# Handing a hand-synchronised section to GpSimd without its drain, and turning the two waits of the last stores

## The chip, the cores and the metric

The kernel runs on one core of one Trainium2 chip. The metric is the time of one execution in microseconds (us) as the device measures it. It was measured in several rounds, each beside the kernel before on the same chip. The time of a run is about 1.75 us more than the span of its trace (575.02 against 573.27 in the profiled run of the kernel before). In the records shown here, us and ns count from the start of the span.

## The reference

With a 1x1 depthwise kernel, the program is a scale per channel followed by a matrix product over 147,456 pixels of 384 channels:

```python
# x: (1, 384, 384, 384) bf16, dw: (1, 1, 384), pw: (384, 384)
out = x * dw[0, 0][None, None, None, :]
return jnp.einsum('bhwc,cd->bhwd', out, pw)
```

## The kernel before

The scale is folded into the weights at the start (the "head"): a 0/1 selection matrix times `dw`, then matmuls with `pw` (line 243), then six evictions into `w_r` (line 299; an eviction copies matmul results out of `ps`, where TensorE leaves them). After that TensorE runs 288 supertiles of 48 matmuls each in one loop (line 193). VectorE transposes x ahead of it, ScalarE evicts the results behind it, and SyncE issues nearly all loads and stores. Everything stands in one section in which the author sets every semaphore by hand:

```python
    with tc.tile_critical():                      # line 104: entry and exit of the section
        ...
        def store(t, k):
            ...
            if first + 1 == NS:                   # the last supertile: two half stores
                je = first
                part = slice(2 * D * k, 2 * D * k + 2 * D)
                nc.sync.wait_ge(s_a[je % 2], je // 2 + 2 + k)   # ScalarE's quarter
                nc.sync.wait_ge(s_d, k + 1)                     # VectorE's quarter, line 143
                nc.sync.dma_start(dst[:, part], src[:, part]).then_inc(s_o[g % NR], 16)
                return
```

The head keeps TensorE busy with matmuls on zeros, and repeats some folding matmuls. Both are there only to raise TensorE's clock in time:

```python
        nc.tensor.wait_ge(s_zero, 1)
        idle_work(3)                              # 12 matmuls on zeros
        ...                                       # three tiny matmuls that spread dw
        idle_work(3)
        nc.tensor.wait_ge(s_pw, 16)
        times = {(1, 1): 3, (2, 0): 2}            # repeats of the folding pairs (k, r)
        for k in range(3):
            nc.tensor.wait_ge(s_sw, k + 1)
            for r in range(2):
                if k == 2:
                    nc.tensor.wait_ge(*w_done[r])
                for v in [0, 1] * times.get((k, r), 1):
                    mm = nc.tensor.matmul(...)    # line 243
                mm.then_inc(s_w)                  # releases one eviction into w_r
```

The last supertile's eviction is shared by two engines:

```python
            if jj + 1 == NS:
                nc.vector.wait_ge(s_o[g % NR], ...)     # an older store of this buffer
                nc.vector.wait_ge(s_pe, 2 * jj + 2)     # the matmuls
                nc.scalar.wait_ge(s_pe, 2 * jj + 2)
                for q in (0, 2):
                    nc.scalar.copy(Ov[:, q, j, :], PS[s][:, q, :D]).then_inc(s_a[s])
                    nc.vector.tensor_copy(Ov[:, q + 1, j, :], PS[s][:, q + 1, :D]).then_inc(s_d)
```

## Time and profile before

| what | before |
|---|---|
| time, median of the first 3 runs | 575.13 us (575.04 to 575.19) |
| head: start to the loop's first matmul | 6.98 us |
| loop: first to last matmul's start | 561.46 us |
| tail: last matmul's start to the end of the span | 4.84 us |
| last store's landing to the start of GpSimd's exit barrier | 0.707 us |

Read it as three pieces one after the other. The loop is TensorE at work without a gap, so a change that doesn't touch it can only win in the head or in the tail. The profile lines for this stand in the prediction. The finer steps come from the trace's records of single sequencer instructions; each gives a start in ns.

### The profile page before, as it was taken

The numbers are of one execution on the slowest core, as the hardware profiler recorded it, in microseconds if no ns is written. First come the engines' busy times: TensorE is split into PE (matmuls) and PEld (weight loads), VectorE is DVE, ScalarE is ACT, GpSimd is POOL, SyncE is SP. The second block draws the span as 40 slices with busy tenths as digits, with TensorE's granted clock in tenths as the row PEclk, the third lists the DMA queues.
The fourth block names the chain that finished last, engine by engine and source line by source line (L and its number), as shares of the span: only waits on it lengthen the run. The fifth ranks groups of instructions, "written<-read, shape, count | busy, mean of one in ns | idle before, by whom it ended". The sixth has DMA issues, their size and how long they took to land.

```text
span 573.3 us, 29723 instructions
## 1 busy us (share of the span) xinstructions
PE 566.7 (99%) x13869; PEld 411.9 (72%) x13869; DVE 507.4 (89%) x584; ACT 419.0 (73%) x297; POOL 0.9 (0%) x8
## 2 busy tenths in 40 slices
PE   8999999999999999999999999999999999999996
PEld 5777777777777777777777777777777777777774
DVE  7898898898889889889888988988988898898895
ACT  6777777777777777777777777777777777777775
POOL 0000000000000000000000000000000000000000
PEclk9999999999999999999999999999999999999999
DMA  9999999999999999999999999999999999999676
GB/s 363 418 340 438 415 425 432 446 412 425 428 413 412 406 389 427 402 379 405 431 389 397 412 416 386 406 409 416 406 391 422 405 394 396 424 398 368 263 288 238
DMA packets 26453, 226.88 MB, mean 396 GB/s; under 512 B 1226, under 2 KB 6987, under 8 KB 22603
## 3 DMA queue, kind: packets, MB, share of 16 engines
q1 hardware_dynamic: 25264, 225.61, 97.1%
q10 hardware_dynamic: 1178, 1.18, 0.6%
q14 instruction: 10, 0.07, 0.0%
q8 instruction: 1, 0.02, 0.0%
HBM read 113.54 MB, written 113.25 MB: 396 GB/s over the span
## 4 chain that ended last, share of the span: by engine, by line
PE 97%; DMA 1%; ACT 1%; DVE 0%; issue 0%; SPq 0%
PE ps L193 97%; DMA pw_n<-in_pw_dram 1%; DMA out_dram<-O 0%; ACT w_r L299 0%; ACT O L336 0%; DVE O L334 0%; PE ps L243 0%; SPq L369 0%; SPq L104 0%
## 5 line engine op out<-in xcount | busy, mean ns | idle before, releaser
L193 PE MATMUL ps<-w_r,T 32*128 32x384 bf16 x13824 | 561.8, 321 | 0.5 <-ACT w_r L299 0.5
L286 DVE STREAM_TRANSPOSE T<-X 128x384 uint32<-128x384 uint32 x572 | 500.7, 877 | 55.4 <-DMA X<-in_x_dram 0.3
L336 ACT CAST O<-ps 128x1536 bf16<-128x1536 f32 x287 | 413.0, 1439 | 147.1 <-PE ps L193 147.1
L193 PEld LDWEIGHTS ps<-w_r,T 32*128 32x128 bf16 x13824 | 410.0, 93 | 152.3 <-issue 0.9
L299 ACT CAST w_r<-ps 128x768 bf16<-128x768 f32 x5 | 3.6, 819 | 1.1 <-PE ps L243 1.1
L210 PE MATMUL ps<-zero 32*128 32x384 bf16 x24 | 2.6, 494 | 1.4 <-POOL zero L259 1.4
L286 DVE STREAM_TRANSPOSE T<-Xl 128x384 uint32<-128x384 uint32 x4 | 3.5, 877 | 0.4
L334 DVE CAST O<-ps 128x384 bf16<-128x384 f32 x2 | 1.0, 553 | 3.1 <-DMA out_dram<-O 3.1
L271 ACT ACT_TABLE_LOAD x1 | 1.3, 1283 | 1.9 <-issue 1.9
L210 PEld LDWEIGHTS ps<-zero 32*128 32x128 bf16 x24 | 0.7, 99 | 2.6 <-issue 2.6
L243 PE MATMUL ps<-pw_n,sel_w 64*128 64x384 bf16 x18 | 2.3, 422 | 0.1
L243 PEld LDWEIGHTS ps<-pw_n,sel_w 64*128 64x128 bf16 x18 | 1.0, 121 | 1.4 <-issue 0.7
L304 DVE TENSOR_REDUCE sel<-eye 128x64 f32<-128x128 bf16 x1 | 0.3, 290 | 1.8 <-POOL eye L261 1.8
L299 DVE CAST w_r<-ps 128x768 bf16<-128x768 f32 x1 | 1.0, 958 | 1.0 <-PE ps L243 1.0
L333 ACT CAST O<-ps 128x384 bf16<-128x384 f32 x2 | 0.9, 482 | 0.5 <-PE ps L193 0.5
L314 DVE TENSOR_SCALAR sel_w<-sel,dw_f 128x256 bf16<-128x256 f32 x3 | 0.9, 347 | 0.0
L311 DVE COPY dw_f<-ps 128x3 f32<-128x3 f32 x1 | 0.2, 161 | 0.7 <-PE ps L225 0.7
L225 PEld LDWEIGHTS ps<-ones,dw_row 1*128 1x128 bf16 x3 | 0.2, 98 | 0.2 <-issue 0.2
L261 POOL TENSOR_SCALAR_AFFINE_SELECT eye<-ones 128x128 bf16<-128x128 bf16 x1 | 0.3, 294 | 0.1
L271 ACT COPY warm<-warm 128x1 f32<-128x1 f32 x2 | 0.3, 189 | 0.0
L259 POOL MEMSET zero<- 128x192 uint32 x1 | 0.3, 258 | 0.0
L225 PE MATMUL ps<-ones,dw_row 1*128 1x1 bf16 x3 | 0.2, 160 | 0.0
(6 smaller groups left out, 0.7 us busy)
## 6 DMA issues: line engine op xcount, KB each, us to landing
X<-in_x_dram SPq DMA_DIRECT2D x26, 3840.0 KB, 21.5
out_dram<-O SPq DMA_DIRECT2D x26, 3840.0 KB, 27.4
X<-in_x_dram SPq DMA_DIRECT2D x3, 1536.0 KB, 17.5
out_dram<-O SPq DMA_DIRECT2D x4, 768.0 KB, 9.3
out_dram<-O SPq DMA_DIRECT2D x2, 1536.0 KB, 14.6
X<-in_x_dram SPq DMA_DIRECT2D x3, 768.0 KB, 7.3
X<-in_x_dram SPq DMA_DIRECT2D x1, 2304.0 KB, 19.2
out_dram<-O SPq DMA_DIRECT2D x1, 2304.0 KB, 10.9
```

The lines of the kernel that those rows point to most:

```text
L193: mm = nc.tensor.matmul(PS[s][:, q, :D], lhsT=Ts[s][32 * q : 32 * q + 32, b, par::2], rhs=w_r[32 * q : 32 * q + 32, b, par, :], start=(b, ...
L210: nc.tensor.matmul(PS[0][:, i, :D], lhsT=zero[32 * i : 32 * i + 32, 0:P], rhs=zero[32 * i : 32 * i + 32, :], start=True, stop=True, tile_p ...
L225: mm = nc.tensor.matmul(PS[1][:, 0, D + k : D + k + 1], lhsT=dw_row[:, P * k : P * k + P], rhs=ones[0:1, 0:1], start=True, stop=True,)
L243: mm = nc.tensor.matmul(PS[(k + 1) % 2][:, 2 * r + v, :D], lhsT=sel_w[64 * v : 64 * v + 64, k, r, :, :].rearrange("p q w -> p (q w)"), rhs ...
L259: nc.gpsimd.memset(zero[:].bitcast(U32), 0).then_inc(s_zero)
L271: c = nc.scalar.copy(warm[:, s + 1 : s + 2], warm[:, 0:1])
L286: ins = nc.vector.transpose(out=Tw[:, 3 * h : 3 * h + 3], in_=Xw[:, :, j, 96 * h : 96 * h + 96].rearrange("p k (b w) -> p b k w", w=32),)
L299: o = nc.vector.tensor_copy(out, in_) if e == 0 else nc.scalar.copy(out, in_)
L314: nc.vector.tensor_scalar_mul(sel_w[:, k], sel[:].unsqueeze(2).to_broadcast([P, 2, 4, 32]), dw_f[:, k : k + 1]).then_inc(s_sw)
L333: nc.scalar.copy(Ov[:, q, j, :], PS[s][:, q, :D]).then_inc(s_a[s])
L334: nc.vector.tensor_copy(Ov[:, q + 1, j, :], PS[s][:, q + 1, :D]).then_inc(s_d)
L336: a = nc.scalar.copy(Ov[:, :, j, :], PS[s][:, :, :D])
```

## The change

The intent is to take synchronisation off the end of the program. GpSimd, idle after 2 us, becomes the section's synchronising engine, the one that announces the section's end and collects the answers. Its drain at the section's end is left out; a drain is the instruction with which an engine answers such an announcement. Of the two waits ahead of each last half store, the one for VectorE (which finishes last) is to be the one that the store itself carries.

```diff
-    with tc.tile_critical():
+    with tc.tile_critical(sync_engine=mybir.EngineType.Pool, no_gpsimd_drain=True):
...
                 part = slice(2 * D * k, 2 * D * k + 2 * D)
+                nc.sync.wait_ge(s_d, k + 1)
                 nc.sync.wait_ge(s_a[je % 2], je // 2 + 2 + k)
-                nc.sync.wait_ge(s_d, k + 1)
                 nc.sync.dma_start(dst[:, part], src[:, part]).then_inc(s_o[g % NR], 16)
```

The built program puts the wait written first at the store and the other one in an instruction ahead of it.

## The prediction

> **What bounds the kernel now.** I read the page first, then the chain of waits in order of time, then the records of the first 7 us and the last 5 us one instruction at a time, because the change touches only instructions at the two ends of the program.
>
> The page says which engine sets the length:
>
> ```profile
> span 573.3 us, 29723 instructions
> PE 566.7 (99%) x13869; PEld 411.9 (72%) x13869; DVE 507.4 (89%) x584; ACT 419.0 (73%) x297; POOL 0.9 (0%) x8
> PEclk9999999999999999999999999999999999999999
> PE 97%; DMA 1%; ACT 1%; DVE 0%; issue 0%; SPq 0%
> ```
>
> TensorE is busy for 99% of the span at the full granted clock, and 97% of the chain that ended last is TensorE. GpSimd does 0.9 us of work, all of it in setup. The chain in order of time then splits the span into three parts:
>
> ```profile
> 0.79 0.01 SPq L104
> ...
> 0.86 0.03 SPq L369
> ...
> 1.02 3.02 DMA pw_n<-in_pw_dram
> ...
> 4.09 0.52 PE ps L243 x2
> ...
> 4.63 2.21 ACT w_r L299 x3
> ...
> 6.98 557.90 PE ps L193 x13728
> ...
> 568.88 1.01 DVE O L334 x2
> ```
>
> Columns: start, length, what. There is a head of 6.98 us (a marker on SyncE's sequencer, then a branch that waits for it, then the load of the weights, their folding, two evictions); 557.90 us of the matmul loop in one piece, to which the chain view adds the last supertile (TensorE's last matmul ends near 568.76); and a tail of about 4.5 us. No line of the loop is touched by the diff. So the question is only how the head and the tail move, each at most a few tenths of a microsecond.
>
> The tail, from the timeline (start, length, engine, what):
>
> ```profile
> 568.80 0.86 ACT L333 CAST O<-ps 128x384 bf16<-128x384 f32 x2 [0.51 <-PE ps L193]
> 568.87 1.02 DVE L334 CAST O<-ps 128x384 bf16<-128x384 f32 x2 [3.09 <-DMA out_dram<-O]
> 569.52 0.82 SPq L144 DMA_DIRECT2D out_dram<-O  x2
> ```
>
> ScalarE and VectorE evict two quarters each, and SyncE stores them in two halves. VectorE ends later. ("DMA out_dram<-O" as the releaser of VectorE is the view's choice among two waits; that buffer's older store had landed long before, the matmuls released it.) The section's boundary is line 104:
>
> ```profile
> L104 SPq EVENT_SEMAPHORE  x3: 17/27/28, 572.2 to 572.4; - x3
> L104 SPq NOP  x2: 13/16/18, 0.8 to 572.5; - x2
> L104 POOLq DRAIN  x1: 41/41/41, 572.2 to 572.2; - x1
> L104 SPq DRAIN  x1: 7/7/7, 572.3 to 572.3; - x1
> ```
>
> Numbers are ns (least, median, most), then first and last start. The reader should see that GpSimd's drain takes 41 ns and starts together with those of the other engines.
>
> The records of single instructions, in ns resolution, give the steps I use below. SyncE's tail: wait for VectorE's first quarter 569.460, store 569.518 (344 ns); wait for the second 569.924, store 569.978; its last byte lands 571.948; the wait for it ends 571.971; branch 572.013; then the boundary: signal 572.178, drain 572.271, two waits 572.350 and 572.420, NOP 572.486, end drain 572.559, second end drain 572.622, which lets GpSimd's exit barrier go at 572.655. From its start there 0.62 us of barrier and semaphore clearing follow.
>
> **What the Trainium skill says.** "Perfetto Trace Analysis", Sequencer-only Instruction (DRAIN, etc): a record covers execution alone; the wait and the propagation of a semaphore lie outside. The trace agrees: the signal at 572.178 lasts 17 ns, and ScalarE's drain that waits for it starts at 572.217, 22 ns after. So I count starts to starts, not busy times. The same page, Identifying Dependency Chains, says that an instruction that waits on several engines may get EventSemaphore instructions ahead of it: here, the second wait of each last store is such a record on SyncE, line 143. "VectorE: DVE Perf Modes", The DRAIN you can't avoid, calls the drains of pre- and postamble constant at about 12 ns; here 7 to 17 ns on four engines and 41 ns on GpSimd, so GpSimd's is dearer but small. "DMA: Bandwidth & Descriptors", Anatomy of one DMA, gives a fixed cost near 2.0 us per DMA (fitted on GpSimd's path); the last store takes 1.97 us here, and the change leaves it alone: only its start can move.
>
> **The change part by part.** The instruction order shows no difference on TensorE, VectorE and ScalarE apart from which semaphore releases their boundary; only GpSimd and SyncE change.
>
> 1. *The two last stores.* In the kernel before, the built program has VectorE's wait in the separate instruction and ScalarE's at the store, the reverse of the source order; the changed source turns this round. VectorE is the late one: its first quarter ends 568.874 + 0.558 = 569.432, ScalarE's at 569.284. Now the store starts 569.518 - 569.432 = 86 ns after VectorE, of which 58 ns are from the separate wait to the store. With VectorE's wait at the store itself the wait for ScalarE is served early. A store that waits at itself shows what is left: the one at line 147 starts at 568.319, some 20 ns after its eviction. So 569.455, about 60 ns earlier. The second half: VectorE ends 569.897, and SyncE, 62 ns (gap 569.862 to 569.924) after the first store, is free at 569.80 + 0.06 for ScalarE's wait and at 569.92 for the store, just as VectorE's signal arrives. So about 569.92 instead of 569.978. Gain 0.055 us, straight on the path: landing and all after it follow.
>
> 2. *The exit.* Before, SyncE announces the end of the section, every engine drains and answers, SyncE collects. In the changed program GpSimd announces, right after its setup at about 2 us; the others answer as soon as each ends its own work (TensorE near 568.8, the evictors near 569.9). When SyncE comes out of its branch at 572.178 its drain finds the announcement already there. It saves the announcement: 572.271 - 572.178 = 93 ns. Then SyncE executes two waits (added by the compiler) and the end drain; before, two waits, a NOP and the end drain. It saves the NOP: 66 to 73 ns. New sum on SyncE: drain 572.178, then 79 + 70 + 66 + 63 ns by the same gaps, second end drain at 572.456 instead of 572.622: 0.165 us. GpSimd's part runs beside it: its wait sees SyncE's drain at about 572.21, its NOP about 66 ns later, the signal back at 572.32, before SyncE's end drain at 572.393 asks for it. That is a margin of 70 ns. The GpSimd drain itself gives nothing: it ended 572.261, and SyncE asked for it at 572.486.
>
> 3. *The entry.* Before, GpSimd's release of the start barrier (0.680) goes to SyncE (0.721), whose NOP (0.786) releases all branches; SyncE's own branch follows at 0.862 and its first load at 1.020. In the change GpSimd runs the NOP itself at about 0.680 + 0.07 = 0.75, the signal is out near 0.79, and SyncE, with one instruction less, reaches its branch at 0.786. So its branch starts 0.07 us sooner. That load (the weights) heads the chain: landed 4.04, first folding matmul 4.09. TensorE had been waiting since 3.87, so it can follow by 0.07; ScalarE's three evictions follow one another from there; the first transpose ends 6.684, 150 ns before the last eviction that the loop waits for (6.833), so it doesn't take over. ScalarE's load of x moves by only 0.03. Gain 0.07 us if the load's landing does not wander.
>
> Sum: 0.055 + 0.165 + 0.07 = 0.29 us of 575.13, 0.05%.
>
> **The rivals.** (a) A new wait replaces the old: GpSimd answers slower than SyncE, or SyncE's two added waits come on top. For it: five of the sequencer steps now lie on GpSimd, whose waits (572.655 to 572.733, 79 ns) are a little longer than SyncE's. Against it: 70 ns of margin. If it eats the exit gain, 575.0; if the added waits cost their whole 0.14 us with nothing saved, 575.15. (b) The entry gain vanishes, since the loop's start hangs on a DMA landing whose 16 parts are spread over 3.669 to 4.040, and on the clock's rise in the head (first full-speed record at 5.57): 574.9. (c) The drain of GpSimd hides more than its record shows: as its name in the change suggests, someone expected a gain. Nothing in the trace supports it (one 41 ns record, off the path); it would bring 574.7. (d) A big effect in the loop, through another phase of loads against stores: TensorE has 0.5 us of recorded idle time before the loop's matmuls in all, so there is nothing to win, and the loads run ahead by three buffers, so I see nothing to lose.
>
> **Range and chances.** 575.13 - 0.29 = 574.84. The three runs of before spread over 0.15 us, as large as any one of my terms; the low end takes all gains plus that spread, the high end takes no gain at all: 574.55 to 575.15. A 2% step is 11.5 us, more than head and tail together could give short of removing both, so "within 2%" is all but certain; I leave 0.015 for a state or a mechanism that I don't see.
>
> **What would show it.** Right: the loop's first matmul near 6.91 instead of 6.98; the first of the two last stores within 30 ns of the end of VectorE's first quarter, with the wait of line 143 served before that; from the last landing to GpSimd's exit barrier 0.54 us instead of 0.71; the drain of line 104 gone from GpSimd, and TensorE's drain of that line near 568.9. Wrong: a SyncE end drain that starts late after its waits (GpSimd's answer binds), a weights load that starts earlier but lands no sooner, a second store that starts no earlier although the first did, or any difference in the length of the matmul loop larger than these 0.29 us.

## The result, and the profile after

| | before | changed |
|---|---|---|
| median of 6 runs | 575.12 us | 575.02 us |
| lowest to highest | 575.04 to 575.70 | 574.78 to 576.34 |
| ratio | | 1.0001 (0.9988 to 1.0014) |

Ratios here are the mean time of one kernel's fast runs over that of the other's of the same rounds, so not quite the ratio of the medians. Within 2% it is the same, as forecast. Of the forecast 0.29 us, the medians show 0.10 and the means nothing, and two of the six runs (575.43, 576.34) lie above the forecast range, which ended at 575.15. The 0.10 is no sign of the gain: six runs with this scatter can give such a difference by chance.

The page of the changed kernel looks the same at the top:

```profile
span 573.2 us, 29725 instructions
PE 566.9 (99%) x13869; PEld 415.0 (72%) x13869; DVE 508.0 (89%) x584; ACT 419.0 (73%) x297; POOL 0.9 (0%) x8
```

The chain of waits in order of time (start, length, what) is another one in the head:

```profile
0.76 0.01 POOLq L104
...
1.14 0.20 POOL zero L259
...
1.45 1.36 PE ps L210 x12
...
2.88 1.17 PE ps L210 x12
4.05 2.05 PE ps L243 x12
6.09 0.02 issue
6.12 0.81 ACT w_r L299
6.92 0.14 issue
7.06 557.91 PE ps L193 x13728
```

Before, the chain ran over the weights' load (3.02 us), two folding matmuls (0.52) and three evictions of ScalarE in a row (2.21). Now the view takes it over TensorE's own warm-up matmuls and twelve folding matmuls (2.05), and only one eviction is on it. Its part before the folding is a matter of the view: the folding again started 47 ns after the weights' landing, as before. The part after it is real. The loop starts at 7.06 instead of 6.98 although the load came sooner: it was issued at 0.954 instead of 1.020 and landed at 3.956 instead of 4.040, and the first folding matmul started at 4.003 instead of 4.087. Somewhere between folding and loop 0.17 us were lost (3.058 us instead of 2.890).

In the tail the steps came out as worked out. The timeline (start, length, engine, what):

```profile
568.89 0.86 ACT L333 CAST O<-ps 128x384 bf16<-128x384 f32 x2 [0.51 <-PE ps L193]
568.96 1.02 DVE L334 CAST O<-ps 128x384 bf16<-128x384 f32 x2 [3.09 <-DMA out_dram<-O]
569.54 0.84 SPq L144 DMA_DIRECT2D out_dram<-O  x2
```

Everything is 0.085 us later than before (568.89 for 568.80), but the store only 0.027 (569.545 for 569.518). The instructions of line 104 (engine, kind and count, then least/median/most ns, then first and last start):

```profile
L104 POOLq NOP  x3: 13/13/13, 0.8 to 572.3; - x3
...
L104 PEldq DRAIN  x1: 1072/1072/1072, 567.8 to 567.8; - x1
L104 ACTq DRAIN  x1: 892/892/892, 568.9 to 568.9; - x1
L104 DVEq DRAIN  x1: 1009/1009/1009, 569.0 to 569.0; - x1
L104 SPq DRAIN  x1: 7/7/7, 572.2 to 572.2; - x1
```

GpSimd's drain is gone. The drains of the other engines now start while they are still at their last work: those of TensorE, ScalarE and VectorE take some 0.9 to 1.1 us, where before all stood at 572.2 and took 8 to 17 ns. The time of a drain is not a cost in itself; it lies beside the stores. By single records:

| step | before | forecast | changed |
|---|---|---|---|
| VectorE's first quarter ends, to the first half store | 86 ns | 20 to 30 | 28 |
| VectorE's second quarter ends, to the second half store | 81 ns | about 25 | 28 |
| last landing to GpSimd's exit barrier | 707 ns | about 540 | 535 |
| last matmul's start to the end of the span | 4.837 us | 4.62 | 4.632 |

So the tail won 0.205 us of the 0.22 that were forecast. The head gave 0.084 back instead of winning 0.07, which leaves 573.27 - 573.15 = 0.12 us in the two spans.

### The profile page after: what moved, and what is told of

Read it like the earlier page. It is cut to its first block, busy times and chain, and to the rows that moved or that the text cites. A ratio compares the mean times of both kernels' runs of the same rounds, so it can differ in the third digit from the quotient of the medians.

```text
span 573.2 us, 29725 instructions
## 1 busy us (share of the span) xinstructions
PE 566.9 (99%) x13869; PEld 415.0 (72%) x13869; DVE 508.0 (89%) x584; ACT 419.0 (73%) x297; POOL 0.9 (0%) x8
## 4 chain that ended last, share of the span: by engine, by line
PE 98%; DMA 0%; ACT 0%; issue 0%; DVE 0%; DVEq 0%; POOL 0%; POOLq 0%
PE ps L193 97%; PE ps L210 0%; DMA out_dram<-O 0%; PE ps L243 0%; ACT O L336 0%; ACT w_r L299 0%; DVE O L334 0%; DVEq L104 0%; POOL zero L259 0%; POOL warm L258 0%; PE ps L225 0%; POOLq L369 0%; POOLq L358 0%; POOLq L104 0%
```

## The experiments

**The theories.** A: the head's length hangs on when TensorE's full clock is granted (the trace records from when to when it was; I call the start of that record the clock's rise). The record of the granted clock begins at 5.57 us in the profile of before and at 5.92 in that of the change; both last 566.612 us, which is 166 times 3.4133 us; in the other profiles here it lasts 563.199, 570.026 or 573.439 us, so whole steps of 3.413. The Trainium skill, "TensorE: Matmul & The Clock Gate", Part 1: The HAM clock gate (the "warmup" mystery), says that the clock is released after a busy window of 3413 ns, and that the window is free-running: it doesn't reset when a kernel starts. The granted stretches agree. If so, the rise is a matter of chance in each run, and its scatter covers a gain of 0.2 to 0.3 us. B: the scatter comes from transfers or from the loop. C: GpSimd gives back elsewhere what it wins. D: what is won is the drain.

### The stretched head: e1 and e2

To take the chance out, the head was made some 4.7 us longer, so that the clock is up before the folding begins. VectorE's first reduction runs 16 times, each waiting for the one before; TensorE's second warm-up loop has 16 passes.

```diff
-        nc.vector.tensor_reduce(out=sel[:], ...).then_inc(s_dwf)
+        for n in range(16):
+            ins = nc.vector.tensor_reduce(out=sel[:], ...)
+            if n > 0:
+                ins._wait_ge(s_pad, n)
+            ins.then_inc(s_pad if n < 15 else s_dwf)
...
         mm.then_inc(s_df)
-        idle_work(3)
+        idle_work(16)
```

e1 is the kernel before with this edit:

> The kernel before with the head stretched by some 4 us: 16 small VectorE reductions in a row instead of one hold the folding back, and TensorE's second warm-up loop has 16 passes instead of 3, so that the full clock is granted before the folding matmuls begin. Theory A (the head's length depends on when the full clock is granted: 5.57 us in the profile of before, 5.92 in that of the change, and in other runs later; that scatter covers a gain of 0.2 to 0.3 us): the slow outliers go, all runs lie within 0.3 us of each other, at 578 to 581 us, and the loop's matmuls again take 561.46 us first start to last start. Theory B (the scatter comes from transfers or from the loop): the scatter stays at 0.6 us and more.

e2 is the changed kernel with it:

> The same stretched head in the changed kernel. Theory A: within 0.3 us of each other, and below the stretched kernel before by 0.22 us (the exit's 0.165 and the stores' 0.055; the entry's 0.07 is hidden behind VectorE here, whose start is the same in both). Theory B: the two can't be told apart, or differ by less than 0.1 us. Rival C (GpSimd as the synchronising engine gives back elsewhere what it wins): the changed one is no faster, 0 +- 0.05.

Measured: e1 579.70 us, five runs from 579.69 to 579.70. e2 579.51, four runs from 579.50 to 579.51 and one at 579.73. In the same rounds the unstretched kernel before scattered from 574.90 to 575.58. The clock rose at 7.77 and 6.76 us, one us apart, and it made no difference: from the first folding matmul to the loop 2.724 and 2.723 us, the loop 561.460 and 561.461. In the chain of e2, again three evictions stand in one row ahead of the loop:

```profile
8.62 0.34 PE ps L211 x4
8.96 0.01 issue
8.98 0.35 PE ps L244 x2
9.33 0.02 issue
9.35 2.21 ACT w_r L300 x3
11.57 0.14 issue
11.70 557.90 PE ps L194 x13728
```

Of theory B the loop falls, with its transfers: there nothing scatters. The loads of the head are not tested by this, since the stretch hides them as it hides the clock's rise: the weights landed at 3.995 and 3.924 us, the folding began at 8.944 and 8.979. So A fits, but these two runs alone don't part it from late loads; e10 and the table after e16 do. C falls: the change wins 0.19 us. Its parts by trace are 0.226 us in the tail (VectorE's last end to the exit barrier 2.775 and 2.549 us) less 0.034 in the head, because the loop starts at 11.702 instead of 11.668. The stretched head hangs on TensorE's warm-up loop of 16 passes: its last four matmuls (8.62, line 211) stand right ahead of the folding, while VectorE had the first selection matrix ready at 7.457, so the 16 reductions didn't bind. That loop begins 0.029 later (1.456 for 1.427), because GpSimd now runs the section's NOP before it clears the zeros. The announcement in the middle of GpSimd's setup adds nothing (the instruction after it starts 0.031 later, the one before it 0.030). The start I had put down as "same" (0.22 expected). The run at 579.73, like e5's at 579.77 below, left no trace and stays unexplained.

### The parts without the stretched head: e3 and e4

```diff
 # e3: the kernel before with the new section line alone
-    with tc.tile_critical():
+    with tc.tile_critical(sync_engine=mybir.EngineType.Pool, no_gpsimd_drain=True):
 # e4: the changed kernel with the old section line
```

> Only the section's synchronising engine and drain are changed, the order of the last waits is as before. By step: from the last landing to the exit barrier's first GpSimd wait 0.535 us (as in the change; 0.707 before); the last stores start 86 and 81 ns after VectorE's quarters (as before). Theory A: the time depends on the clock's rise in each run; the fastest run 0.24 us under the fastest of before (574.80), the median anywhere within 0.4 us of before. Rival C: the fastest run not under 575.0.

> Only the order of the last waits is changed, the section is as before. By step: the last stores start 28 ns after VectorE's quarters instead of 86 and 81; landing to exit barrier 0.707 us as before. Theory A: fastest run 0.05 us under the fastest of before (574.99), medians again not to be told apart. Rival C makes no difference here: the same.

Measured: e3 575.14 us (574.72 to 575.28), ratio 0.9997; e4 575.08 (574.88 to 576.10), ratio 1.0003. By time nothing is to be seen, as theory A has it; the fastest runs lay 0.08 and 0.11 under what was expected of them, and e3's, at 574.72, under the 575.0 of rival C. By step all came as expected: e3 0.535 us from landing to barrier and stores 87 and 82 ns after VectorE; e4 0.706 us and 28 and 27 ns.

### The parts with the stretched head: e5 to e8

Each with the stretched head: the section line alone (e5), the order of the waits alone (e6), the kernel before without GpSimd's drain (e7), the changed kernel with GpSimd's drain (e8).

```diff
 # e7, on the stretched kernel before
-    with tc.tile_critical():
+    with tc.tile_critical(no_gpsimd_drain=True):
 # e8, on the stretched changed kernel
-    with tc.tile_critical(sync_engine=mybir.EngineType.Pool, no_gpsimd_drain=True):
+    with tc.tile_critical(sync_engine=mybir.EngineType.Pool):
```

> Stretched head (before 579.70 us, changed 579.51), with only the section's engine and drain changed. Theory A, by the traces of those two: the exit gives 0.17, the section's start on GpSimd costs VectorE's first reduction 0.034 (its input comes from GpSimd, which now has one more instruction ahead of it): 579.70 - 0.17 + 0.034 = 579.56, within 0.03. Rival C (the exit gains nothing by itself, the stores' order does it): 579.70 or more.

> Stretched head, with only the order of the last waits changed. Theory A: the last store starts 28 ns after VectorE instead of 82, so 579.70 - 0.055 = 579.645, within 0.03. Rival (SyncE's own time between two stores binds, so the second store doesn't start earlier): 579.70. The sum of this and the section's run must give the whole change's 0.19 if the parts are independent.

> Stretched head; SyncE stays the synchronising engine, only GpSimd's drain is left out (a NOP takes its place). Theory A: the drain of 41 ns ended 0.2 us before SyncE asked for it: 579.70, within 0.02. Rival D (the drain is what the change pays for): 579.50 to 579.60.

> Stretched head; the whole change but for the drain, which GpSimd keeps. Theory A: GpSimd reaches it right after its setup near 2 us and no one waits for it at the end: 579.51 as the changed one, within 0.02. Rival D: 579.65 to 579.70.

| stretched kernel | median | lowest to highest of 5 |
|---|---|---|
| before (e1) | 579.70 | 579.69 to 579.70 |
| order of the waits alone (e6) | 579.64 | 579.63 to 579.65 |
| section line alone (e5) | 579.55 | 579.54 to 579.77 |
| both: the change (e2) | 579.51 | 579.50 to 579.73 |
| before without GpSimd's drain (e7) | 579.69 | 579.68 to 579.71 |
| the change with GpSimd's drain (e8) | 579.50 | 579.48 to 579.52 |

The parts add up: 0.06 + 0.15 = 0.21 against 0.19 for both. Leaving the drain out changes the time by 0.01, down in one pair and up in the other, so theory D falls. That the gain comes from who announces and closes the section shows in the records of its lines. In e7 SyncE still announces, and a NOP took the drain's place in the same instant, 576.9:

```profile
L105 POOLq NOP  x1: 13/13/13, 576.9 to 576.9; - x1
L105 DVEq DRAIN  x1: 17/17/17, 576.9 to 576.9; - x1
...
L105 SPq DRAIN  x1: 7/7/7, 577.0 to 577.0; - x1
```

In e2 GpSimd announced at 1.5 us, and the others answered when their work was done:

```profile
L105 POOLq EVENT_SEMAPHORE  x3: 17/43/43, 1.5 to 576.9; - x3
...
L105 DVEq DRAIN  x1: 1007/1007/1007, 573.7 to 573.7; - x1
L105 SPq DRAIN  x1: 7/7/7, 576.9 to 576.9; - x1
```

### The clock in the head: e9 and e10

e9 leaves both warm-up loops out; e10 leaves the repeats of the folding out.

```diff
 # e9
         nc.tensor.wait_ge(s_zero, 1)
-        idle_work(3)
...
         mm.then_inc(s_df)
-        idle_work(3)
 # e10
-        times = {(1, 1): 3, (2, 0): 2}
+        times = {}
```

> The changed kernel without TensorE's warm-up matmuls in the head (both loops left out), so that TensorE's first real work is the folding near 4.0 us. Theory A: the full clock comes later than 7.1 us, the loop starts at half clock near 7.1, and is longer than 561.46 us by half of the time from its start to the clock's rise: a rise at 7.5 to 10.9 gives 0.2 to 1.9 us, times of 575.1 to 576.8, scattered by 0.5 us and more. Theory B (the clock in the head doesn't matter): 574.8 to 575.2 as the changed kernel's faster runs, loop 561.46.

> The changed kernel without the six repeated folding matmuls ((1,1) three times and (2,0) twice in the table of repeats become once). Theory A: at half clock these repeats hold back the third of ScalarE's weight evictions (6.118 us instead of 5.93 in the profile of the change); without them the evictions follow one another at 0.69 us and the loop starts at 6.89 to 6.92 even if the clock rises at 6 us or later: 0.15 us earlier than in the profile of the change, and the fastest runs at 574.7. Rival E: the repeats are what brings the clock up in time; without them it rises a window (some 3.4 us, the spacing that the records show is 566.612 us over 166) later, and the loop grows by up to 1.7 us: median above 575.3.

e9 took 575.25 us (574.74 to 576.20). The scatter came as expected, though two of the five runs (574.74, 574.95) lie under the forecast of 575.1 to 576.8. In the profiled run, its fastest, the clock rose at 6.62 us, before the loop: the expectation "later than 7.1" missed, and its loop was 561.461 us. So the clock can rise before the loop without the warm-up matmuls too, and this run tells nothing of a loop at half clock.

e10 does. Of its six runs three took 574.67 to 574.68, the others 576.60, 576.91 and 580.88. The profile is of the run at 576.60: the clock rose only at 10.82 us. The folding ran at half clock throughout, and yet the loop started 2.890 us after it, at 6.865. But the loop took 563.382 us. The matmuls of the loop in e10 (least/median/most ns):

```profile
L193 PE MATMUL ps<-w_r,T x13824: 321/321/523, 6.9 to 570.2; 32*128 32x384 bf16 x198
```

and in the kernel before:

```profile
L193 PE MATMUL ps<-w_r,T x13824: 318/321/332, 7.0 to 568.4; 32*128 32x384 bf16 x198
```

The median is the same; some matmuls of e10 took 523 ns. A table by stages shows where. Its columns are the stage, its length, busy time and count of each engine, granted clock, DMA share and rate. e10:

```profile
6.80:10.80 4.00, 3.94 (x52) 2.31 (x56) 2.77 (x4) 1.33 (x2) 0.00 (x0) 1.00 1.04 436
10.80:14.80 4.00, 4.00 (x104) 2.71 (x100) 3.51 (x4) 2.88 (x2) 0.00 (x0) 1.00 1.09 460
```

and the kernel before:

```profile
6.80:10.80 4.00, 3.82 (x96) 2.85 (x100) 4.00 (x6) 2.88 (x4) 0.00 (x0) 1.00 1.03 429
10.80:14.80 4.00, 4.00 (x107) 2.91 (x103) 3.61 (x5) 2.88 (x2) 0.00 (x0) 1.00 1.03 433
```

The first number in brackets counts matmuls: 52 against 96 in the same 4 us, with TensorE equally "busy" and the clock printed as 1.00 in both. The clock's record starts with the rise, so what lies before it isn't counted. Count the matmuls there, not the column.

Both halves of theory A are in this. The repeats at half clock hold ScalarE's third eviction back. In the profile of the change the pair that releases it ended at 5.581 + 0.494 = 6.075 us, and the eviction started at 6.118; ScalarE would have been free for it at 4.545 + 2 x 0.69 = 5.93. In the profile of before the clock was up in time, the same pair ended at 5.945, and ScalarE was free at 6.016. If the clock comes later than the loop's start, the loop pays on top, about half of the delay: (10.82 - 6.865) / 2 = 1.98 us, measured 563.382 - 561.460 = 1.92. Rival E is supported too: without the repeats two of six runs were late by 1.9 and 2.2 us (576.60 and 576.91), and the one of them with a trace shows a late clock. So the repeats seem to earn their place; six runs are few. (The run at 580.88, and one at 580.13 in e11, had a mean granted clock of 0.994 against 0.998 to 1.000 in the others. They have no trace, and I leave them open.)

### A better order on VectorE: e11 and e12

VectorE's last eviction has the same trouble as the stores had: its wait for the matmuls, which comes last, stands in an instruction of its own ahead of it.

```diff
-                nc.vector.wait_ge(s_o[g % NR], ...)
                 nc.vector.wait_ge(s_pe, 2 * jj + 2)
+                nc.vector.wait_ge(s_o[g % NR], ...)
```

> The changed kernel with the same turn of waits on VectorE as on SyncE: of its two waits before the last evictions the one for the matmuls comes to stand at the eviction itself. By step: its first eviction starts some 5 ns after ScalarE's instead of 69, both stores some 60 ns earlier after the last matmul. In time it is hidden by the clock's scatter: fastest run 574.65 to 574.8, median 574.7 to 575.3.

> That turn in the changed kernel with the stretched head (579.51), where the scatter is gone: 579.45 within 0.02 if VectorE's end sets both stores, 579.50 if SyncE's time between the two stores binds.

Measured: e12 579.42 us (579.41 to 579.43), 0.09 under the stretched change, somewhat more than the 0.06 expected. In the trace VectorE starts 1 ns after ScalarE instead of 69, and both stores 70 ns sooner. e11: 574.60 to 574.61 in four of six runs, 574.96 and 580.13 in the others; its fastest run and its median (574.60) lie under what was expected.

### Moving the repeats: e13 to e16

Here the cause of the lost entry was still open. One of the repeats is moved behind the pair that releases ScalarE's third eviction, so that the count of matmuls stays 18.

```diff
-        times = {(1, 1): 3, (2, 0): 2}
+        times = {(1, 1): 2, (2, 0): 3}
```

e13 is the kernel before with it, e14 the change, e15 the change with e11's turn on VectorE; e16 is the change unaltered.

> The kernel before with one repeat of the folding pair (1,1) moved to the pair (2,0): 2 and 3 passes instead of 3 and 2, the same 18 matmuls. Theory A (repeats at half clock hold back the third of ScalarE's evictions): the loop starts 2.89 us after the folding's first matmul whether the clock rises at 5.6 or at 6.8 us, and the profile's loop is 561.46 us or longer by half of what the rise comes later than the loop's start. Fastest run 574.9 as the fastest of before, fewer runs at 575.1 to 575.2. Rival: the loop starts 3.05 us and more after the folding as before.

> The same in the changed kernel. Theory A: 2.89 us from folding to loop, folding at 3.98 to 4.00, loop at 6.87 to 6.89; fastest run 0.22 to 0.29 us under the fastest of e13, 574.62 to 574.68. If the entry's gain is real on average the difference of the fastest is near 0.27, if the load's landing eats it, 0.2 (exit and stores alone).

> That, and the turn of VectorE's two waits (0.09 us in the stretched kernel): fastest run 574.53 to 574.6, at least three of five runs under the fastest of before (574.88). Late rises of the clock still give single runs above 575.

> The changed kernel again, unaltered. Theory A: fastest run 574.7 to 574.8, scatter of 0.5 us and more above it; in the profile the loop starts 2.89 us after the folding if the clock rises within 1.5 us of the folding's start, 3.05 to 3.09 if later; loop 561.46 us, longer only if the rise comes after the loop's start.

Measured: e13 575.04 us (574.93 to 575.52), e14 575.13 (574.87 to 575.28), e15 574.61 (574.58 to 575.18), e16 574.88 (574.68 to 575.93); the kernel before beside them 575.08 (574.92 to 575.55). e14's fastest run missed its expectation by 0.2: five runs are too few for a comparison of fastest runs under this scatter. The traces say more than the times:

| profiled run | clock's rise | folding | loop | folding to loop | loop's length |
|---|---|---|---|---|---|
| before | 5.57 | 4.087 | 6.977 | 2.890 | 561.460 |
| e13 (before, moved repeats) | 5.50 | 4.103 | 6.995 | 2.892 | 561.460 |
| changed | 5.92 | 4.003 | 7.061 | 3.058 | 561.460 |
| e4 | 6.14 | 4.001 | 7.090 | 3.089 | 561.460 |
| e16 (changed again) | 6.30 | 3.981 | 7.066 | 3.085 | 561.460 |
| e11 | 6.33 | 4.144 | 7.231 | 3.087 | 561.461 |
| e3 | 7.53 | 3.988 | 7.072 | 3.084 | 561.662 |
| e15 (moved repeats) | 7.08 | 4.560 | 7.450 | 2.890 | 561.460 |
| e14 (moved repeats) | 7.88 | 3.990 | 6.985 | 2.995 | 561.874 |
| e10 (no repeats) | 10.82 | 3.975 | 6.865 | 2.890 | 563.382 |

The rise orders the unaltered heads: up to 5.57 us it takes 2.89 us from folding to loop, from 6.1 us on 3.08 to 3.09, whichever engine synchronises (e9, without warm-up matmuls but with the repeats: 6.62 and 3.088). With the repeats moved, e15 takes 2.890 though its clock rose 2.5 us after the folding's start. In e14 another limit came in: a late load of x, whose first transpose ended at 6.851. Where the rise comes after the loop's start the loop grows by about half of the difference (e14: 0.45 worked out, 0.41 measured; e3: 0.23 and 0.20). e15 also shows a second source of chance: the one-row load of `dw` landed at 3.10 us instead of 2.2, and the folding began half a microsecond late. The weights' landing is a third: from 3.798 (e9) to 4.098 us (e11) over these profiles, and e9 aside the folding it released began between 3.975 (e10) and 4.144 (e11). How the scatter of the times divides between clock and loads the runs don't show.

e15 had four of five runs at 574.58 to 574.65, below every one of the 44 runs of the kernel before (574.88 to 575.96). So had e11 in four of six, and these few runs don't tell the two apart. The ratio of e15, 0.9992 (0.9978 to 1.0005), still can't be told from 1 at five runs.

## Why the prediction was right or wrong

**What bounds it, and the loop untouched: right.** The loop took 561.460 us in both profiles, and 561.46 in every run whose clock was up at its start.

**The last stores: right.** 58 and 53 ns were won for the 55 forecast; alone it is worth 0.06 us of time (e1, e6).

**The exit: right.** 0.172 us for the 0.165 forecast. The drain itself is worth nothing (e7, e8), as the step said; what counts is that SyncE no longer makes the announcement at the end (0.093 from signal to drain) nor runs the closing NOP (0.072), which GpSimd runs beside SyncE's two waits. The two shares are read from the records; no run parts them.

**The entry: wrong, and this is the step that failed.** The prediction put "Gain 0.07 us if the load's landing does not wander", on the ground that "ScalarE's three evictions follow one another from there". That is what failed. In the profile of the change the load was issued 0.066 sooner and landed 0.084 sooner, the folding followed, and still the loop started 0.084 later: at half clock the repeated folding matmuls ended only at 6.075, and ScalarE's third eviction waited for them until 6.118 instead of following at 5.93. Between folding and loop that cost 0.17. Where the repeats were left out (e10) or one of them was moved behind that eviction's release (e15), the evictions did follow one another, and from folding to loop it was 2.890 us again, under a clock that rose later still.

Smaller errors sit in the same term. The chain counts three evictions, where the prediction's reading of it says two. "TensorE had been waiting since 3.87" isn't so: where the load landed at 3.832 (e10) and at 3.902 (e16) the folding started at 3.975 and 3.981, 143 and 79 ns after the landing, while in the profiles with landings from 3.942 on it started 45 to 48 ns after them (e15, which waited for `dw`, aside), and in e9, which has no warm-up matmuls, 46 ns after a landing at 3.798. So TensorE's own warm-up matmuls seem to hold it until about 3.98, and they begin 0.023 later under GpSimd (1.452 for 1.429), since GpSimd runs the NOP before it clears the zeros. The entry's gain has a floor, and where the warm-up matmuls lead, as in the stretched head, it is a loss of 0.034. What it is worth on average in the unstretched kernel the runs don't settle. Nor do they settle whether the change itself lets the clock rise later: without the stretch it rose at 5.50 to 6.14 us in the three profiles with SyncE and at 5.92 to 7.88 in the six with GpSimd and all warm-up work; with the stretch there is no such order (5.66 to 7.77 and 5.18 to 7.73).

**Rival (b): named, and mis-sized.** It had the clock's rise and would have made the time 574.9. The rise costs up to 0.2 us in the head, and half of any delay past the loop's start on top: 1.92 us in e10. The range took the scatter of three runs of before (0.15 us) for that of the kernel. 44 runs of it scatter over 1.08 us, 11 of the change over 1.66.

**The rivals (a), (c) and (d): rightly rejected.** GpSimd's answer came in time (its NOP at 572.346, SyncE's end drain at 572.442), and the drain and the loop gave nothing.

So the change is a real but small gain: 0.19 us where the clock and the first loads are taken out of play. In the kernel as it is, 11 runs of the change have their median at 574.89, 44 of before at 575.115, while their means are equal to a hundredth (575.16), because two of the 11 lie at 575.93 and 576.34. No trace was taken of those two; that a late clock makes them is inferred from e10, not shown.

## What to carry to other kernels

A wait that ends last belongs on the instruction that needs it, and the built program may turn the order in which you wrote the waits: check which of them stands ahead, since a separate one costs about 55 ns after the last signal. An end-of-section handshake is cheaper, here by 0.17 us, when an idle engine announces and closes it and the others answer as they finish. And before you hunt for tenths of a microsecond, take the run-to-run chance out of the program (here by holding the work back until the clock is up and the first loads are in): that brought the scatter from 0.7 us to between 0.01 and 0.04 (one run in five of e2 and of e5 aside) and made parts of 0.06 measurable.

## What the Trainium skill lacked or had wrong

- "TensorE: Matmul & The Clock Gate", Part 1: The HAM clock gate (the "warmup" mystery), has the transition around 4 us into sustained matmul activity, plus or minus 500 ns. Its free-running window of 3413 ns fits the granted stretches here (566.612 us is 166 of them). But with the first matmuls at 1.43 to 1.46 us, the rise came between 5.18 us (e5) and 7.88 us (e14) with warm-up matmuls and repeats in the head, and at 10.82 us without repeats: 3.7 to 9.4 us into an activity that has gaps.
- The same section calls the ramp's penalty less than 1% of a typical span. That holds here, with up to 1.92 us in the loop (0.33%); but it is more than six times the forecast gain of 0.29 us, so it can't be left out where tenths of a microsecond are compared.
- "VectorE: DVE Perf Modes", The DRAIN you can't avoid, has drains of pre- and postamble at about 12 ns, constant. It doesn't speak of a section's own drains. Where an engine reaches such a drain while its last work still runs, the record lasts until that work is done: 892 ns on ScalarE, 1009 ns on VectorE, 1072 ns on TensorE in the changed kernel (ScalarE's last eviction ended at 569.750, its drain at 569.789).
- No page has the cost of a wait in an instruction of its own after the last signal: 86 and 81 ns from VectorE's end to the store, against 28 with that wait on the store.
